# First QKV groups of a four-layer transformer kernel: two row blocks that share weight chunks, batch statistics, earlier border zeros, and a new table of half-steps

## Chip, cores and metric

The kernel runs on one core of one Trainium2 chip. The metric is device time in microseconds (us), taken as the median of several executions. Before the change the three shown executions took 1742.13, 1744.40 and 1746.95 us, so the median is 1744.4 us.

## What is computed

Four layers are applied one after another to x, a matrix of 2048 rows and 640 columns in float32. Layers 0 and 2 are of kind A (attention over eight earlier rows at a stride of 2, 32 heads of 20), layers 1 and 3 of kind B (a Fourier mix over rows and columns, written as matrix products).

```python
x = A_x
x = x + _A_ref(_layernorm(x), A_wqkv, A_wo)
x = x + _B_ref(_layernorm(x), seq_re, seq_im, hid_re, hid_im)
x = x + _A_ref(_layernorm(x), A_wqkv, A_wo)
x = x + _B_ref(_layernorm(x), seq_re, seq_im, hid_re, hid_im)
# _A_ref: qkv = x @ wqkv; softmax over 8 gathered keys; weighted values; @ wo
# _B_ref: seq_re @ (x @ hid_re.T) - seq_im @ (x @ hid_im.T)
```

## The kernel before

Rows are cut into 16 blocks of 128, four chunks c of four blocks j. Every float32 product is made of three passes of fp32r operands (`PASSES`, line 324): each operand is split into a rounded part, hi, and a rest, lo, and the passes are hi·hi, hi·lo and lo·hi. So a split costs a cast and a subtraction for each tile (`split`, line 228; on ScalarE, VectorE or GpSimd), and a group of QKV (one row block by up to 512 columns, 5 chunks k of 128 along the depth) costs 15 matmuls (`qkv_mm`, line 467). A row block gets there by normalisation, five 128x128 transposes on TensorE (`t_pe`, line 327), a cast out of PSUM (`t_hi`, line 336) and a subtraction (`t_lo`, line 340).

`layer_a` (line 348) is ordered by hand on all five engines: a plan of steps -8 to 66 (half-steps: half of a unit of attention each), and in each step a list of phases. The table `CFG` gives for each piece of work its step, and `ph` the order of the phases. Attention products run on VectorE (lines 557, 570, 600) and GpSimd (lines 560, 615 to 617), two half-steps for each of 32 units; TensorE fills in QKV groups, transposes of attention outputs (line 442), subtraction of the hi part in PSUM by a matmul with a negative identity (line 450, `pc_sub`), output products (line 640) and, as the layer runs out, the first products of the next B layer (line 1123, `z_mm`, 15 matmuls for one slab of c, in thirds of 5 that the table `z` places). The B layers' slabs come raw (`cst_in`, transposed on TensorE into `aux` banks) or as they are (`cs_in`). `ln_lo` (line 1046) makes the lo part of the normalised rows of the B layer on VectorE or GpSimd, as the bits `lnv` say.

Before any of that, 18 bf16 matmuls on zeros run on TensorE (line 206). The start of layer 0 is `prologue_first` (line 743). It loads x block 0, weight chunks 0 to 2 of the first QKV group of columns, x block 1, chunks 3 and 4, x blocks 2 and 3, and then the weights of the other three column groups in large pieces (lines 674 and 310), all on the SyncE queue. Then a string `pro` gives the order of small steps: `s` statistics of a block (lines 246 to 252, 274, 280: a reduction on VectorE, squares on ScalarE, a power on GpSimd), `n` normalise (line 293), `H` and `L` hi and lo of a weight chunk (lines 759 and 762; the letter names the engine), `p`, `h`, `l` transposes, cast and subtraction of block 0. The blocks 1 to 3 are transposed in the middle of the groups before them (`mid`, line 474). The border rows of the key and value buffers are zeroed by `zero_rows` (line 736) in the middle of group 1.

Of the kernel before, what the change touches and what calls it, by code (L numbers as in the profile page):

```python
# [13 lines left out]
AF = mybir.ActivationFunctionType  # L14
# [6 lines left out]
D = 640  # L21
# [15 lines left out]
CFG = {'pro': 's0 H0a H2a H1a L0v n0v L1g p0 h0 L2g s1 H3v H4v l0 L3v L4v s2 n1v',  # L37
 'mid0': 's3 n2v',
 'mid0n': 0,
 'mid1': 'n3v',  # L40
 'mid1n': 0,
# [12 lines left out]
 'pad2': 16,  # L54
 'ot': ['ot'],
 'wqg': [0, 0, 0, 0, 0, 0, 0, 1, 1, 1, 0, 1, 0, 1, 1, 0, 1, 0, 1, 0],
 'run': [{'pre': [0, 1, 2, 0, 1, 0, 2, 0, 0, 0, 0, 2, 0, 1, 0, 0],
          'post': [5, 1, 1, 2, 1, 4, 0, 5, 0, 7, 0, 3, 0, 4, 1, 5],
          'y': [[3, 4, 5, 6, 8], [9, 13, 14, 14, 15]]},
         {'pre': [6, 0, 1, 2, 4, 3, 0, 4, 0, 6, 0, 0, 2, 0, 0, 0],  # L60
          'post': [0, 0, 2, 2, 0, 4, 0, 0, 0, 0, 1, 0, 4, 0, 4, 3],
# [13 lines left out]
         'z': [148, 149, 149, 151, 151, 156, 156, 157, 157, 159, 161, 162, 167, 168, 170, 171, 171, 173, 174, 174,  # L75
               175, 175, 175, 176, 178, 179, 180, 180, 181, 184, 186, 186, 187, 187, 188, 188, 191, 193, 194, 198,
# [4 lines left out]
         't2': [48, 48, 48, 48, 52, 51, 52, 52],  # L81
         't3': [57, 58, 60, 60],
         'wst': [0, 0, 0, 0, 0, 0, 0, -1, 0, 1, 0, 0, -1, 1, 0, 0],
         'kvq': [1, 0, 1, 1, 0, 1, 1, 0, 0, 0, 0, 0, 1, 0, 1, 0, 0, 0, 0, 0, 0, 0, 1, 0, 0, 0, 1, 0, 1, 0, 1, 0],
# [5 lines left out]
         'ph': ['evac dma peT0 pe hi z0 fin peL z1 red0 pe2 qk dma2 sA sB red1 sC av0 loE sD sE exp actl evacA sF '  # L90
                'evacO av1 qc dmaw dmac actL lnl pe3w dmar misc clo dmas pe3',
                'peT0 evac dma pe hi z0 peL red0 pe2 z1 fin qk dma2 sA av0 sD sE sB red1 evacA sC loE actL sF evacO '
                'exp dmac av1 actl qc dmas misc clo lnl dmar dmaw pe3 pe3w'],
# [5 lines left out]
         'lnv': [1, 1, 1, 0, 0, 1, 0, 0, 0, 1, 0, 0, 1, 1, 0, 1],  # L99
# [29 lines left out]
         'zla': [0, 0, 2, 0, 1, 0, 1, 1, 1, 1, 0, 1, 0, 2],  # L129
         'ph': ['dma peT0 evac hi red0 pe z0 peL qk z1 fin sA pe2 red1 dma2 sB sD sC av0 loE sE clo evacA exp actl '  # L130
                'actL sF evacO av1 qc dmaw dmas misc pe3 lnl dmar dmac pe3w',
                'peT0 red0 evac pe z0 dma hi fin peL sA z1 qk dma2 pe2 sB red1 av0 sD loE evacA sC sE exp actL evacO '
                'sF av1 dmas dmaw qc actl dmar lnl misc pe3w clo dmac pe3'],
# [3 lines left out]
         'lno': [False, False, True, True],  # L137
# [3 lines left out]
         'tail': 'z68 P H L M2 z67 M3 A2 S2 F2 c14 d14 p14 T2 A3 l2 Z14 z69 S3 F3 c15 d15 p15 T3 l3 G0 G1 G2 Z15 E '  # L141
                 'e0 h0 k0 e1 e2 e3 e4 h1 k1'}],
 'xcr': ['stg', 'sg3', 'sg3']}
TA = 65
NWARM = 18
STG = (-1, "dma2")
NWIN = CFG['nwin']
ZTAGS = ("m0", "m1", "xt", "t0", "t1")
NT = 8
# [19 lines left out]
def tile_layers(ctx: ExitStack, tc: tile.TileContext, x, wqkv, wo, cs, cst, wre, wim, out):  # L169
# [35 lines left out]
    for i in range(NWARM):  # L205
        nc.tensor.matmul(wb, zero[:, :P], zero[:, :512], start=True, stop=True)
# [1354 lines left out]
```

## Time and profile before

| What | Value |
|---|---|
| median of three executions | 1744.4 us |
| the profiled execution | 1743.01 us |
| its span in the trace | 1741.2 us |
| TensorE matmul busy | 1717.2 us, 99% |
| VectorE busy | 1360.1 us, 78% |
| ScalarE busy | 822.6 us, 47% |
| GpSimd busy | 616.1 us, 35% |
| data moved | 419.91 MB, mean 241 GB/s |

The profiled execution lies 1.8 us above its span and 1.4 us below the median. Shares over the whole span mix stages: in layers 0 and 2 VectorE and GpSimd are as full as TensorE, in layers 1 and 3 GpSimd has next to nothing to do. A row of the timeline has a start, a length, the engine, the line, the operation with output and input tiles, its count, and in brackets the idle time of the engine ahead of it with what ended it. A short idle time of TensorE counts as such; the sum of its rows in this profile is about 20 us.

### The profile page before, as it was taken

To read this page: it belongs to the slowest core of one execution; us is meant where nothing else is said; L and a number is where in the kernel's file an instruction comes from. 1 tells how busy PE (TensorE), PEld (TensorE's weight loads), DVE (VectorE), ACT (ScalarE), POOL (GpSimd) and SP (SyncE) were. 2 spreads that over 40 slices of the span, in tenths; PEclk is the share of its full clock that TensorE was granted. 3 is DMA by queue.
4 is the path that set the end of the run, shared out by engine and by line. 5 is a ranking of instruction groups with operands and counts; after the bars stand their busy time and mean duration, and the time that the engine had idled before them with its cause. 6 is when DMAs were issued, how large, how long until landed. Compare 5 with 4: busy or idle time off the path is not lost. (4 is left out here: it accounts for less than half of the span.)

```text
span 1741.2 us, 26545 instructions
## 1 busy us (share of the span) xinstructions
PE 1717.2 (99%) x8828; PEld 1496.2 (86%) x8828; DVE 1360.1 (78%) x2117; ACT 822.6 (47%) x1810; POOL 616.1 (35%) x574
## 2 busy tenths in 40 slices
PE   9999999999999999999999999999999999999999
PEld 6888888788888888888888889888888888888888
DVE  5999999878767767767639998899787677677673
ACT  5655644654445444445534434445444444443441
POOL 4899999950000000000019997899200000000000
PEclk9999999999999999999999999999999999999999
DMA  6786779969787687687548856698598768867861
GB/s 239 245 291 199 209 231 309 323 222 331 264 262 232 215 275 235 206 279 226 189 156 269 273 163 219 213 312 318 179 349 268 256 205 260 257 208 240 264 203 54
DMA packets 266713, 419.91 MB, mean 241 GB/s; under 512 B 22192, under 2 KB 144560, under 8 KB 266320
## 3 DMA queue, kind: packets, MB, share of 16 engines
q1 hardware_dynamic: 251744, 408.38, 71.1%
q10 hardware_dynamic: 14832, 9.83, 1.8%
q8 instruction: 70, 1.15, 0.3%
q14 instruction: 67, 0.55, 0.1%
HBM read 332.99 MB, written 85.14 MB: 240 GB/s over the span
## 5 line engine op out<-in xcount | busy, mean ns | idle before, releaser
L477 PE MATMUL m<-r,s 128*128 128x512 f32 (+1 forms) x1920 | 429.8, 379 | 1.3 <-DVE r L759 0.8
L477 PEld LDWEIGHTS m<-r,s 128*128 128x128 f32 x1920 | 350.2, 188 | 57.5 <-DVE r L759 1.2
L1284 ACT CAST r<-win 128x512 fp32r<-128x512 f32 x242 | 147.1, 620 | 176.1 <-DVE win L1320 103.2
L1190 PE MATMUL aux<-r2a,zo 128*128 128x320 f32 x768 | 226.0, 309 | 0.0
L557 DVE TENSOR_TENSOR pr<-pq,win 128x1280 f32<-128x1280 f32 x128 | 189.8, 1483 | 37.5 <-PE aux L1190 20.3
L615 POOL TENSOR_TENSOR pr<-pr 128x640 f32<-128x640 f32 x126 | 207.5, 1647 | 30.3 <-DVE pr L600 29.1
L1190 PE MATMUL aux<-pr,zo 128*128 128x320 f32 x704 | 208.0, 309 | 0.0
L560 POOL TENSOR_TENSOR pr<-pr 128x640 f32<-128x640 f32 x123 | 176.3, 1433 | 88.4 <-DVE pr L557 88.4
L1285 DVE TENSOR_TENSOR r<-win,r 128x512 fp32r<-128x512 f32 x242 | 162.8, 688 | 38.5 <-ACT r L1284 37.7
L600 DVE TENSOR_TENSOR pr<-pq,win 128x1280 f32<-128x1280 f32 x128 | 190.3, 1488 | 2.6
L280 POOL TENSOR_TENSOR stats<-stats,mhalf 128x1 f32<-128x1 f32 (+1 forms) x31 | 22.1, 714 | 457.9 <-ACT stats L274 457.8
L1291 PE MATMUL m<-r,r 128*128 128x512 f32 x600 | 152.9, 389 | 0.0
L1190 PEld LDWEIGHTS aux<-r2a,zo 128*128 128x128 f32 x768 | 144.2, 188 | 2.2
L1190 PEld LDWEIGHTS aux<-pr,zo 128*128 128x128 f32 x704 | 132.2, 188 | 2.4
L1291 PEld LDWEIGHTS m<-r,r 128*128 128x128 f32 x600 | 112.2, 188 | 23.5 <-DVE r L1285 0.6
L1291 PE MATMUL t<-r,r 128*128 128x512 f32 x492 | 132.0, 390 | 0.0
L616 POOL TENSOR_TENSOR pr<-pr 128x320 f32<-128x320 f32 x126 | 113.1, 897 | 9.9
L570 DVE TENSOR_REDUCE lg<-pr 128x64 f32<-128x640 f32 (+1 forms) x128 | 107.2, 837 | 10.0 <-POOL pr L560 9.7
L1320 DVE TENSOR_TENSOR win<-win,win 128x512 f32<-128x512 f32 x109 | 74.9, 691 | 48.4 <-DMA win<-cs_in 46.8
L1291 PEld LDWEIGHTS t<-r,r 128*128 128x128 f32 x492 | 92.4, 188 | 19.8
L1123 PE MATMUL m<-s,r 128*128 128x512 f32 x348 | 106.7, 394 | 2.0 <-ACT r L1060 0.9
L1123 PE MATMUL t<-s,r 128*128 128x512 f32 x348 | 105.2, 390 | 0.0
(297 smaller groups left out, 3236.1 us busy)
## 6 DMA issues: line engine op xcount, KB each, us to landing
win<-cs_in SPq DMA_DIRECT2D x346, 256.0 KB, 4.1
r<-xc SPq DMA_DIRECT2D x240, 256.0 KB, 4.2
win<-kvb SPq DMA_DIRECT2D x96, 440.0 KB, 4.7
xa<-cs_in SPq DMA_DIRECT2D x120, 256.0 KB, 4.5
win<-kvb SPq DMA_DIRECT2D x64, 360.0 KB, 6.0
xc<-sg SPq DMA_DIRECT2D x28, 512.0 KB, 4.6
xr<-xs SPq DMA_DIRECT2D x40, 320.0 KB, 3.5
kvb<-stg SPq DMA_DIRECT2D x32, 320.0 KB, 2.7
```

What stands on the lines that cost most here:

```text
L477: nc.tensor.matmul(mt[g][:, : GW[q]], st[:, a, k], wq[q][:, b, k], start=n == 0, stop=n == 14)
L557: nc.vector.tensor_tensor(pr, q, wview(u, jp, 0, [[1, FE]]), op=ALU.mult)
L560: nc.gpsimd.tensor_tensor(pv[:, :, 0:10], pv[:, :, 0:10], pv[:, :, 10:20], op=ALU.add)
L570: nc.vector.tensor_reduce(rows(lgs[u], jp), pv.rearrange("p (a h) d -> p a h d", h=HE), axis=AX.X, op=ALU.add,)
L600: nc.vector.tensor_tensor(pr.rearrange("p j w (h d) -> p (j w) h d", d=DH), rows(lgs[u], jp).unsqueeze(3).to_broadcast([P, 2 * W, HE, DH]) ...
L615: g.tensor_tensor(pr[:, :, 0:4], pr[:, :, 0:4], pr[:, :, 4:8], op=ALU.add)
L616: g.tensor_tensor(pr[:, :, 0:2], pr[:, :, 0:2], pr[:, :, 2:4], op=ALU.add)
L1123: self.last = nc.tensor.matmul(self.z[t][k], self.xn[c][:, a, j, k * P : (k + 1) * P], self.ct[s][:, b], start=s == 0 and i == 0, stop=s = ...
L1190: self.last = nc.tensor.matmul(self.ym[e][:, :320], zt[(k, a, ri)][:, j2 * P : (j2 + 1) * P], w[:, e * 320 : (e + 1) * 320], start=(k, a, ...
L1284: nc.scalar.copy(hi, raw)
L1285: nc.vector.tensor_tensor(lo, raw, hi.bitcast(F32), op=ALU.subtract)
L1291: nc.tensor.matmul(bank, w(a, kb), hl[b], start=start and (a, b) == (0, 0), stop=stop and (a, b) == (1, 0),)
```

## The change

Five things are changed together.

- The prologue loads x blocks 0 and 1 first, then weight chunks 0, 3, 1, 2, 4, then x blocks 2 and 3, then the border zeros, then the large weight pieces (`pld`). The zeros get a tile of their own tag.
- Row statistics of layer 0's first four blocks are made by two `bn_stats` on halves of 320 columns and one `bn_aggr` on VectorE, then Ln and Exp of the variance on ScalarE. The reduction, the squares and GpSimd's power go.
- Groups 0 and 1 (row blocks 0 and 1 with the first column group) are no longer run one after the other: `pro` names each of their 30 matmuls (`m0a` is group 0, pass hi·hi, chunk 0; letters a to e are hi·hi, f to j are x hi by weight lo, k to o are x lo by weight hi).
- 15 matmuls on zeros instead of 18.
- Many numbers of the step tables move by one or so: `gs`, `z`, `out`, `wo`, `ph`, `tail` and others of both A layers, the engine bits `wqg` and `lnv`, and `run` and `y` of the B layers.

TensorE's queue, at the start of the program (`t` and `aux` are PSUM banks of the transposes, `m` those of the groups, `pr` the row blocks, `r` the split weights, `s` the transposed blocks; the number behind a name tells tiles apart). Before:

```order
L331 MATMUL t_33_203<-ident_69,pr_13_158 128x128 x2
L331 MATMUL t_34_206<-ident_69,pr_13_158 128x128 x3
L477 MATMUL m_37_233<-r_0_12_157,s_32_202 128x512 x10
L331 MATMUL aux_39_245<-ident_69,pr_18_167 128x128 x2
L331 MATMUL aux_40_248<-ident_69,pr_18_167 128x128 x3
L477 MATMUL m_37_233<-r_0_12_157,s_32_202 128x512 x5
L477 MATMUL m_44_272<-r_0_12_157,s_38_244 128x512 x10
```

And with the change, on the same queue from the same place on:

```order
L350 MATMUL t_38_215<-ident_69,pr_13_155 128x128 x2
L350 MATMUL t_39_218<-ident_69,pr_13_155 128x128 x3
L350 MATMUL aux_41_224<-ident_69,pr_15_157 128x128 x2
L350 MATMUL aux_42_227<-ident_69,pr_15_157 128x128 x3
L804 MATMUL m_43_242<-r_0_12_154,s_37_214 128x512 x2
L804 MATMUL m_44_245<-r_0_12_154,s_40_223 128x512
L804 MATMUL m_43_242<-r_0_12_154,s_37_214 128x512
L804 MATMUL m_44_245<-r_0_12_154,s_40_223 128x512 x3
L804 MATMUL m_43_242<-r_0_12_154,s_37_214 128x512 x4
L804 MATMUL m_44_245<-r_0_12_154,s_40_223 128x512
```

The transposes of block 1 stand ahead of all matmuls of group 0, and the two groups take turns.

VectorE's queue at the start (`stats`, `bns`, `bna` hold statistics, `win` the raw weight chunks). Before:

```order
L246 TENSOR_REDUCE stats_189<-pr_13_158 128x1
L247 TENSOR_SCALAR stats_189<-stats_189 128x1
L762 TENSOR_TENSOR r_0_12_157<-win_160,r_0_12_157 128x512
L293 TENSOR_SCALAR pr_13_158<-pr_13_158,stats_189 128x640
L246 TENSOR_REDUCE stats_189<-pr_18_167 128x1
L247 TENSOR_SCALAR stats_189<-stats_189 128x1
L759 CAST r_0_12_157<-win_169 128x512
L759 CAST r_0_12_157<-win_171 128x512
```

And with the change, from the same place on:

```order
L260 BN_STATS bns_198<-pr_13_155 128x6 x2
L261 BN_AGGR bna_199<-bns_198 128x2
L260 BN_STATS bns_203<-pr_15_157 128x6 x2
L261 BN_AGGR bna_204<-bns_203 128x2
L270 TENSOR_SCALAR pr_13_155<-pr_13_155,bna_199,stats_185 128x640
L270 TENSOR_SCALAR pr_15_157<-pr_15_157,bna_204,stats_185 128x640
L361 TENSOR_TENSOR s_37_214<-t_38_215,s_37_214 128x256
L361 TENSOR_TENSOR s_37_214<-t_39_218,s_37_214 128x384
```

Both blocks are now normalised before any weight chunk is touched on VectorE; the lo part of chunk 0 has gone to GpSimd.

TensorE's queue near the end of layer 0, where slabs of the next layer (`stg`) and attention outputs (`zo`) are transposed between thirds of `z_mm` (five matmuls each; `wa` and `s` are slabs that are split). Before, transposes first and two thirds behind them:

```order
L442 MATMUL aux_585_3695<-ident_69,zo_520_3259 128x128 x3
L442 MATMUL aux_587_3697<-ident_69,stg_3667 128x128 x4
L1123 MATMUL m_496_3155<-wa_3645,r_1_539_3391 128x512
L1123 MATMUL m_497_3156<-wa_3645,r_1_539_3391 128x512
L1123 MATMUL xt_3157<-wa_3645,r_1_539_3391 128x512
L1123 MATMUL t_499_3158<-wa_3645,r_1_539_3391 128x512
L1123 MATMUL t_500_3159<-wa_3645,r_1_539_3391 128x512
```

With the change, the end of the second of these thirds, and what follows it:

```order
L1162 MATMUL t_512_3186<-wa_3599,r_1_544_3394 128x512
L461 MATMUL aux_590_3708<-ident_69,zo_527_3269 128x128 x3
L461 MATMUL aux_592_3710<-ident_69,stg_3675 128x128 x4
L469 MATMUL aux_590_3708<-s_589_3707,nident_74 128x384
L469 MATMUL aux_592_3710<-s_591_3709,nident_74 128x512
```

The transposes stand two thirds later, and the subtractions (now line 469) follow them at once.

The diff, cut to its core:

```diff
@@ CFG @@
-CFG = {'pro': 's0 H0a H2a H1a L0v n0v L1g p0 h0 L2g s1 H3v H4v l0 L3v L4v s2 n1v',
- 'mid0': 's3 n2v',
...
+CFG = {'pro': 'b0 b1 f0 n0 f1 H0a p0 n1 p1 H1a h0 l0 L0g h1 l1 H2a m0a m0k m1a m0l H4v m1k m1b m1c H3a L1g m0m b2 m0f m0d '
+        'L3g m0c m1o m0b L2v m1d m1l f2 m0e m1f m1m m1n m0o m1e m0g n2 p2 L4v b3 m0i m0j m0h m0n m1i m1h h2 m1g m1j '
+        'f3 n3 l2',
...
- 'pad2': 16,
+ 'pad2': 64,
...
- 'wqg': [0, 0, 0, 0, 0, 0, 0, 1, 1, 1, 0, 1, 0, 1, 1, 0, 1, 0, 1, 0],
+ 'wqg': [0, 0, 0, 0, 0, 0, 0, 0, 0, 1, 0, 1, 1, 1, 1, 0, 1, 0, 1, 0],
...
-         'lnv': [1, 0, 1, 0, 0, 0, 1, 0, 1, 1, 0, 1, 1, 1, 1, 1],
+         'lnv': [0, 0, 1, 0, 0, 0, 1, 0, 1, 1, 0, 0, 1, 1, 0, 1],
...
+ 'nwarm': 15,
+ 'pld': 'x0 x1 k0 k3 k1 k2 k4 x2 x3 z0',
+ 'mid2': 'p3 h3 l3'}
@@ Stats @@
+        def batch(self, j, xt):
+            b = T([P, 2, nc.vector.BN_STATS_DIM], "bns", bufs=2)
+            a = T([P, nc.vector.BN_AGGR_DIM], "bna", bufs=4)
+            for h in range(2):
+                nc.vector.bn_stats(b[:, h], xt[:, h * 320 : (h + 1) * 320])
+            nc.vector.bn_aggr(a, b)
+            self.mv[j] = a
+
+        def batch_fin(self, j):
+            r = self.rstd[:, j : j + 1]
+            nc.scalar.activation(r, self.mv[j][:, 1:2], AF.Ln, bias=eps)
+            nc.scalar.activation(r, r, AF.Exp, scale=-0.5)
@@ zero_rows @@
-            zrow = wtile([4, (W - 1) * FE])
+            zrow = T([4, (W - 1) * FE], "xr")
@@ prologue_first @@
-            for j, (k0, k1) in enumerate(((0, 3), (3, 5))):
-                if j:
+            for j in range(NJ):
+                if j == 1:
                     T([P, CFG["pad2"]], "pad2")
-                x_load(0, j, f"pr{j}")
-                for k in range(k0, k1):
-                    wq[(0, k)] = wq_load1(0, k)
...
+            for t in CFG["pld"].split():
+                n = int(t[1])
+                if t[0] == "z":
+                    zero_rows()
+                elif t[0] == "k":
+                    wq[(0, n)] = wq_load1(0, n)
...
+            def qmm(j, i, k):
+                a, b = PASSES[i]
+                g = j
+                if count[g] == 0:
+                    mt[g] = pt([P, 512], f"m{g % 2}")
+                nc.tensor.matmul(
+                    mt[g][:, : GW[0]], xnT[(0, j, 1)][:, a, k], w0[:, b, k], start=count[g] == 0, stop=count[g] == 14
+                )
+                count[g] += 1
...
-            mid[1] = m[: CFG["mid1n"]] + xt_all(2, "t") + m[CFG["mid1n"] :] + [(zero_rows, ())]
-            mid[2] = xt_all(3, "aux")
+            mid[2] = [(step, (t,)) for t in CFG["mid2"].split()]
```

More of the change, by code (lines that the diff above doesn't have):

```diff
@@ L204, in tile_layers @@
     wb = pt([P, 512], "m1")
-    for i in range(NWARM):
+    for i in range(CFG["nwarm"]):
         nc.tensor.matmul(wb, zero[:, :P], zero[:, :512], start=True, stop=True)
@@ L240, in __init__ @@
             self.done = set()
+            self.mv = {}
             self.sums = st[:, 8:16].rearrange("p (a j) -> p a j", a=2)
@@ L467, in qkv_mm @@
         def qkv_mm(g, cqj):
+            if first and g < 2:
+                return
             c, q, j = cqj
@@ L786, in step @@
                 elif t[0] == "p":
-                    both(lambda c, j, i: xt_pe(c, j, i, f"t{i}"), 0)
+                    both(lambda c, j, i: xt_pe(c, j, i, f"{('t', 'aux')[j % 2]}{i}"), n)
                 elif t[0] == "h":
-                    both(xt_hi, 0)
-                else:
-                    both(xt_lo, 0)
+                    both(xt_hi, n)
+                elif t[0] == "l":
+                    both(xt_lo, n)
+                else:
+                    for x in e:
+                        i, k = divmod("abcdefghijklmno".index(x), KD)
+                        qmm(n, i, k)
             for t in CFG["pro"].split():
                 step(t)
-            m = [[step, (t,)] for t in CFG["mid0"].split()]
-            mid[0] = m[: CFG["mid0n"]] + xt_all(1, "aux") + m[CFG["mid0n"] :]
-            m = [[step, (t,)] for t in CFG["mid1"].split()]
-            mid[1] = m[: CFG["mid1n"]] + xt_all(2, "t") + m[CFG["mid1n"] :] + [(zero_rows, ())]
-            mid[2] = xt_all(3, "aux")
+            assert count[:2] == [15, 15]
+            mid[2] = [(step, (t,)) for t in CFG["mid2"].split()]
             for i in range(KD):
```

103 lines of the change are left out of this document (54 added, 49 removed), and 14 rows, old and new, of the table CFG.

## The prediction, as it went on record

> **What bounds the kernel now.** I read the page's busy times first, then the windows by stage, then all waits of TensorE. The page's chain of work only reaches back to the middle of the span, so the early stages are read from their windows.
>
> ```profile
> PE 1717.2 (99%) x8828; PEld 1496.2 (86%) x8828; DVE 1360.1 (78%) x2117; ACT 822.6 (47%) x1810; POOL 616.1 (35%) x574
> 0.00:10.00 10.00, 8.01 (x27) 3.33 (x27) 4.99 (x12) 6.13 (x14) 3.88 (x13) 1.00 0.85 302
> 10.00:20.00 10.00, 8.17 (x37) 6.10 (x38) 7.47 (x17) 4.98 (x15) 2.55 (x5) 1.00 0.80 321
> 60.00:360.00 300.00, 292.59 (x1563) 258.14 (x1563) 281.20 (x412) 166.56 (x445) 279.04 (x258) 1.00 0.79 261
> ```
>
> TensorE is busy for 1717.2 of 1741.2 us, at a granted clock of 1.00 (the column behind POOL). No edit takes a real matmul away, so only waits can go: the 24 us without work. The first 20 us leave TensorE 3.8 us idle, part of its early busy time being matmuls on zeros. From 60 to 360 us (most of layer 0) VectorE (281.20 of 300) and GpSimd (279.04) are nearly as full as TensorE (292.59): there a shorter wait of TensorE may only make it wait for them.
>
> **The prologue.** The timeline of TensorE up to the first gapless stretch:
>
> ```profile
> 7.72 0.76 PE L331 MATMUL t<-ident,pr 128*128 128x128 f32 x5 [0.37 <-DVE pr L293]
> 8.61 1.21 PE L477 MATMUL m<-r,s 128*128 128x512 f32 x4
> 10.58 1.19 PE L477 MATMUL m<-r,s 128*128 128x512 f32 x4 [0.76 <-DVE r L759]
> 11.97 1.10 PE L477 MATMUL m<-r,s 128*128 128x512 f32 x2 [0.20 <-DVE r L762]
> 14.02 0.77 PE L331 MATMUL aux<-ident,pr 128*128 128x128 f32 x5 [0.94 <-DVE pr L293]
> 18.07 0.71 PE L331 MATMUL t<-ident,pr 128*128 128x128 f32 x5
> 18.53 2.56 PE L477 MATMUL m<-r,s 128*128 128x512 f32 x10
> 21.39 33.44 PE L477 MATMUL m<-r,s 128*128 128x512 f32 x145
> ```
>
> 145 matmuls take 33.44 us, 0.2306 each; five transposes hold TensorE for 18.53 − 18.07 = 0.46. At 21.39 groups 0 to 3 still lack 25 matmuls, so the first column group ends at 21.39 + 25 × 0.2306 = 27.16 us. Its work is 60 × 0.2306 + 4 × 0.46 = 15.7 us; begun at 7.72 it could have ended at 23.4. So 3.7 us are stalls: block 0 alone can't use a chunk before it is split, and block 1 is normalised only at 13.96.
>
> The rows for the new order's times:
>
> ```profile
> 1.31 6.04 PE L206 MATMUL m<-s 128*128 128x512 bf16 x18 [1.31 <-DVE s L203]
> 5.46 1.39 PEld L206 LDWEIGHTS <-s 128*128 128x128 bf16 x7 [0.18 <-issue]
> 3.71 0.82 DVE L246 TENSOR_REDUCE stats<-pr 128x1 f32<-128x640 f32 x1 [2.38 <-DMA pr<-x_in]
> 4.56 0.15 DVE L247 TENSOR_SCALAR stats<-stats 128x1 f32<-128x1 f32 x1
> 283.87 0.48 DVE L258 SCALAR_TENSOR_TENSOR xa<-aux,xa 128x320 f32<-128x320 f32 x1
> 5.70 0.20 ACT L274 ACTIVATE stats<-stats 128x1 f32<-128x1 f32 x1
> 5.81 1.64 ACT L759 CAST r<-win 128x512 fp32r<-128x512 f32 x3
> 7.05 0.61 DVE L293 TENSOR_SCALAR pr<-pr,stats 128x640 f32<-128x640 f32 x1
> 8.19 0.81 ACT L338 CAST s<-t 128x256 fp32r<-128x256 f32 x2 [0.74 <-PE t L331]
> 10.45 0.88 DVE L342 TENSOR_TENSOR s<-t,s 128x256 fp32r<-128x256 f32 x2
> 7.53 2.71 POOL L762 TENSOR_TENSOR r<-win,r 128x512 fp32r<-128x512 f32 x2 [0.97 <-ACT r L759]
> ```
>
> `bn_stats` isn't in this trace. Its bounds are the one-column row (0.15) and the whole 640-column reduction (0.82); I take half of that reduction, 0.42, close to the 320-column row of 0.48. `bn_aggr` I put at 0.15, at most 0.30. A block's statistics then cost 2 × 0.42 + 0.15 = 1.0 us of VectorE, as before (0.82 + 0.15), but the squares on ScalarE and the power on GpSimd go; Ln and Exp cost 2 × 0.20.
>
> What the loads allow, by windows of 1 us (the last column is GB/s, thousandths of a MB per us), and the two rows of the zeros before:
>
> ```profile
> 1.00:2.00 1.00, 0.69 (x2) 0.28 (x3) 0.32 (x2) 1.00 (x1) 0.38 (x4) 1.00 0.35 36
> 2.00:3.00 1.00, 1.00 (x4) 0.31 (x3) 0.00 (x0) 0.41 (x3) 0.00 (x0) 1.00 0.74 242
> 3.00:4.00 1.00, 1.00 (x4) 0.44 (x3) 0.29 (x1) 0.00 (x0) 0.00 (x0) 1.00 1.05 388
> 4.00:5.00 1.00, 1.00 (x4) 0.30 (x2) 0.68 (x2) 0.25 (x1) 0.00 (x0) 1.00 1.05 307
> 5.00:6.00 1.00, 1.00 (x5) 0.45 (x4) 0.00 (x0) 0.97 (x4) 0.01 (x1) 1.00 0.99 353
> 6.00:7.00 1.00, 1.00 (x7) 0.39 (x4) 0.56 (x1) 1.00 (x3) 0.56 (x1) 1.00 1.03 390
> 18.57 0.56 POOL L738 MEMSET win<- 4x560 f32 x1
> 19.15 2.67 SPq L741 DMA_DIRECT2D kvb<-win  x8
> ```
>
> 0.67 MB have moved by 4.0: blocks 0 and 1 (0.33 MB each). Block 0's consumer starts 0.6 us after its bytes at that rate; so block 1 is there at 4.6, chunk 0 at 5.4, chunk 1 (1.44 MB) at 6.9, the last chunk near 8.2. The zeros' memset (0.56) now stands on GpSimd ahead of the identity's last step, which the transposes need only at 6.75. Their eight issues (2.67) move on SyncE ahead of the large loads, to about 4.6 to 7.3; until 9 us the queue still has the same 2.6 MB of blocks and chunks to move, which hides that delay. Without that cover the large pieces land 2.7 us later, and the second column group needs the first of them only at 23.7.
>
> So: statistics of block 0 end at 4.7, of block 1 at 5.7, Ln and Exp of each 0.5 later; block 0 is normalised 5.7 to 6.35, block 1 until 7.0 (before: 7.66 and 13.96). Seven weight loads of the zeros take 1.39, so three fewer end TensorE's warm-up at 7.35 − 0.6 = 6.75; there the transposes of block 0 start, 0.97 earlier than now. ScalarE casts chunks 0 and 1 until 7.5, block 0 until 8.3, block 1 until 9.1, chunk 2 until 9.7, chunk 3 until 10.2. TensorE starts group 0 at 7.95 and then takes a matmul from whichever group has its operands: about 1.2 us of waits until 10 us, none behind. Chunk 4 (VectorE, 10.5), the lo parts (GpSimd 8.3, 9.6 and 11.6; VectorE 12.3 and 13.6) and block 2 (13 us; needed at 13.5) each come before their turn. With 15.7 us of work from 6.75 and 1.2 of waits, the first column group ends at 23.7. **Gain: 27.16 − 23.7 = 3.4 us.** Bounds: `bn_stats` at 0.82 delays block 1 by 1.6 and more `bn_aggr`, 0.3 more, leaving 1.5; at 0.15 the warm-up holds the transposes at 6.75 anyway, and with every stall gone the gain is 0.97 + 3.7 = 4.7. The first attention product waits for the same groups, so VectorE's and GpSimd's long stretch shifts with TensorE.
>
> **The step table.** Waits of TensorE whose cause the new order moves:
>
> ```profile
> 87.20 0.50 PE L450 MATMUL xt<-s,nident 128*128 128x512 f32 x1 [0.68 <-ACT s L446]
> 108.39 0.66 PE L442 MATMUL xt<-ident,xa 128*128 128x128 f32 x4 [0.92 <-ACT xa L297]
> 287.33 0.66 PE L442 MATMUL aux<-ident,zo 128*128 128x128 f32 x4 [0.46 <-ACT wa L465]
> 325.94 0.63 PE L442 MATMUL aux<-ident,stg 128*128 128x128 f32 x4 [1.69 <-DMA stg<-cst_in]
> 334.95 0.50 PE L450 MATMUL aux<-s,nident 128*128 128x512 f32 x1 [0.68 <-ACT s L446]
> 1156.88 0.50 PE L450 MATMUL aux<-r,nident 128*128 128x256 f32 x2 [1.57 <-ACT r L446]
> ```
>
> At 87.20 and 334.95 a group or a third now stands between transposes and subtraction; at 287.33 a third stands ahead of the transposes; at 325.94 they stand two thirds (2.3 us) later, longer than the load was late. Together 0.68 + 0.46 + 1.69 + 0.68 = 3.5. At the moved place of 325.94 the subtraction follows its transposes at once, as at 334.95 before: 0.68 back, with a third of `z_mm` queued behind it on TensorE and, behind that, nothing but TensorE's own stream. So 2.8. The waits at 108.39 and 1156.88 (2.5 together) also lose their neighbours, but both end with ScalarE's queue, which follows VectorE there: I count nothing. Bounds: nothing, since VectorE and GpSimd are as full; and all 6.0.
>
> **Sum.** 3.4 + 2.8 = 6.2. The profiled execution's 1743.0 (1741.2 of span and 1.8 around it) becomes 1736.8; the median lies 1.4 higher, so 1738.2. Pads, tags and other moved numbers I put at nothing: they change neither the count of matmuls nor any row above, and small waits both ways are inside the bounds.
>
> **Rivals.** Those about VectorE and GpSimd rest on these rows:
>
> ```profile
> 1140.00:1160.00 20.00, 17.95 (x102) 15.46 (x101) 19.04 (x29) 9.66 (x30) 18.98 (x19) 1.00 0.95 322
> L1048 POOL TENSOR_TENSOR r<-r,r x10: 1569/1578/1589, 307.9 to 1201.2; 128x640 fp32r<-128x640 f32 x10
> L759 DVE CAST r<-win x2: 591/1054/1518, 8.5 to 9.0; 128x512 fp32r<-128x512 f32 x2
> ```
>
> - *The table gains nothing.* TensorE's saved waits come back as waits for VectorE or GpSimd at the end of each A layer. For it: both near 94% from 60 to 360 us. Against: the removed waits end with ScalarE or a load. Only the prologue's 3.4 stay: 1741.0.
> - *The table gains all 6.0*: 9.4 off, 1735.0.
> - *GpSimd becomes the bound in layer 2, and the kernel is slower.* `lnv` moves three lo parts there from VectorE to GpSimd at 1.58 us each, 4.7 in all. At 1140 to 1160 GpSimd has 1.0 us free in 20, so three within some 80 us just pass what is free (about 4). It decides once that free time can't be used, because GpSimd's idle moments are waits for VectorE. If the last attention outputs then wait for all of it and the table gains nothing, 4.7 − 3.4 = 1.3 us slower: 1745.7. Against: VectorE, the fuller one (19.04), is relieved.
> - *VectorE and GpSimd get in each other's way in the prologue.* Two casts on VectorE beside GpSimd's subtraction took 0.59 and 1.52, so an overlap can cost 0.93. With the change three subtractions on GpSimd lie beside VectorE's statistics; three such delays, 2.8, leave 0.6 of 3.4 there: 1741.0.
>
> The Trainium skill ("SBUF — State Buffer", "Who interferes with whom") says that the two engines share a port pair which one of them locks for a whole instruction. By that rule the last rival holds wherever VectorE's instruction takes both pairs; the cast of 1.52 agrees, no row here shows it for `bn_stats`. By the rule the time would be 1741.0, by the forecast's reading, in which those instructions run beside each other, 1738.2.
>
> **How the numbers follow.** Forecast 0.55; table nothing 0.18; table all 0.13; prologue collisions 0.06; GpSimd bound 0.08. Two terms' bounds give 1744.4 − 10.7 = 1733.7 to 1744.4 − 1.5 = 1742.9; a median of three whose runs lie 4.8 apart adds about one each way: **1732.5 to 1744.0**. A measurement tells 0.3%, 5.2 us, from no change. The forecast lies 1 us past that edge: two thirds of its chance, all of "table all" and little of the rest make faster 0.52; slower by that needs 8.6 us of losses against the 3.4: 0.04; within, 0.44.
>
> **What would show it.** Right: the gapless stretch of groups begins near 16 us and the first column group ends near 23.7; `bn_stats` near 0.42; no wait for the raw slab near 323; the first attention product 3.4 earlier. Wrong: chunk 1 later than 7.5, `bn_stats` near 0.8, the layer-1 products starting no earlier than the prologue's gain allows, or GpSimd full up to the end of layer 2.

## The result, and the profile after

| Kernel | median, us | range, us | executions | ratio to before, 95% interval |
|---|---|---|---|---|
| before | 1742.65 | 1741.54 to 1746.95 | 7 | |
| changed | 1737.14 | 1736.35 to 1740.75 | 7 | 0.9967 (0.9957 to 0.9976) |
| changed, once more | 1738.08 | 1736.95 to 1738.33 | 6 | 0.9968 (0.9955 to 0.9980) |

The change gains 5.5 us by the first comparison, 0.33%. The forecast was 1738.2, a gain of 6.2 us: 1.1 us above the measured median and inside the range of 1732.5 to 1744.0. Its base, the median of three (1744.4), lies 1.75 us above that of seven.

The first profiled execution of the changed kernel was the slowest of its seven, 1740.75 us. The repeat's profiled execution took 1736.95 us, so I read the terms from that one and call it the second trace. (The profiled execution of the run with the table alone took 1825.91 us at a mean granted clock of 0.889; it is left out of the comparisons, and its trace isn't read.) Its TensorE in the prologue, to be held against the timeline that the prediction shows:

```profile
1.31 4.79 PE L206 MATMUL m<-s 128*128 128x512 bf16 x15 [1.31 <-DVE s L203]
6.47 0.74 PE L350 MATMUL t<-ident,pr 128*128 128x128 f32 x5 [0.37 <-DVE pr L270]
7.11 0.77 PE L350 MATMUL aux<-ident,pr 128*128 128x128 f32 x5
8.17 5.69 PE L804 MATMUL m<-r,s 128*128 128x512 f32 x22 [0.30 <-ACT s L357]
...
17.80 22.42 PE L498 MATMUL m<-r,s 128*128 128x512 f32 x97
```

The matmuls on zeros end at 6.10, and TensorE waits 0.37 us for block 0. Both blocks are transposed one behind the other, 22 matmuls of the two groups follow, and at 17.80 the first four groups lack 25 matmuls, as before at 21.39. At 22.42/97 = 0.231 us each the first column group ends at 23.58 (before 27.16). VectorE in the same stretch:

```profile
3.72 0.89 DVE L260 BATCH_NORM_STATS2 bns<-pr 128x6 f32<-128x320 f32 x2 [2.40 <-DMA pr<-x_in]
4.64 0.21 DVE L261 BATCH_NORM_AGGREGATE bna<-bns 128x2 f32<-128x12 f32 x1
...
5.76 1.30 DVE L270 TENSOR_SCALAR pr<-pr,bna,stats 128x640 f32<-128x640 f32 x2
...
10.13 0.88 DVE L260 BATCH_NORM_STATS2 bns<-pr 128x6 f32<-128x320 f32 x2
...
11.18 0.95 DVE L790 TENSOR_TENSOR r<-win,r 128x512 fp32r<-128x512 f32 x1
...
12.57 0.68 DVE L790 TENSOR_TENSOR r<-win,r 128x512 fp32r<-128x512 f32 x1
```

`bn_stats` takes 0.44 (half of 0.89) and `bn_aggr` 0.21; both blocks are normalised by 7.06 (before 7.66 and 13.96).

Next, one and the same place of TensorE's stream in both traces, first in that of before, then in the second trace:

```profile
58.66 0.50 PE L450 MATMUL xt<-s,nident 128*128 128x512 f32 x1 [0.68 <-ACT s L446]
374.32 2.18 PE L640 MATMUL aux<-r2a,zo 128*128 128x320 f32 x12 [0.46 <-ACT zo L446]
1232.60 2.18 PE L640 MATMUL aux<-r2a,zo 128*128 128x320 f32 x12 [0.46 <-ACT zo L446]
```

```profile
54.94 0.50 PE L469 MATMUL xt<-s,nident 128*128 128x512 f32 x1 [0.68 <-ACT s L465]
369.55 2.17 PE L661 MATMUL aux<-r2a,zo 128*128 128x320 f32 x12 [0.46 <-ACT zo L465]
1226.30 2.17 PE L661 MATMUL aux<-r2a,zo 128*128 128x320 f32 x12 [0.46 <-ACT zo L465]
```

The lead is 3.72 us behind the prologue, 4.77 at layer 0's last output products, 6.30 at those of layer 2, and 6.0 in the spans (1741.2 and 1735.2). So in this pair of traces the prologue gave 3.7 us, the table 1.05 in layer 0 and 1.5 in layers 1 and 2; how far other traces bear that out stands near the end. Where the first 1.05 comes from, and what it was reduced by, stands in the waits of the second trace:

```profile
101.98 5.47 PE L498 MATMUL m<-r,s 128*128 128x384 f32 x30 [1.55 <-ACT sg L513]
301.56 0.66 PE L461 MATMUL aux<-ident,stg 128*128 128x128 f32 x4 [1.55 <-DVE r L277]
1151.65 0.38 PE L469 MATMUL aux<-ot,nident 128*128 128x256 f32 x1 [0.38 <-ACT ot L465]
1158.25 4.66 PE L661 MATMUL aux<-r2a,s 128*128 128x320 f32 x30 [1.08 <-DVE r L277]
```

All the waits that the prediction named are gone or shrunk (at 87.20, 108.39, 287.33, 325.94, 334.95, and 1156.88 from 1.57 to 0.38 at 1151.65). The wait of 0.68 us that the prediction put back behind the moved transposes of the raw slab isn't there either: the subtraction starts at 324.50 with none. Two others have come: 1.55 us at 102, where none was, and 1.55 at 302, where before had 0.22. The second is read from two engines at the same place. Before:

```profile
299.94 4.56 PE L640 MATMUL aux<-r2a,s 128*128 128x320 f32 x30
304.17 0.48 DVE L258 SCALAR_TENSOR_TENSOR r<-aux,r 128x320 f32<-128x320 f32 x1
```

and in the second trace:

```profile
295.35 4.66 PE L661 MATMUL aux<-r2a,s 128*128 128x320 f32 x30
301.02 0.48 DVE L277 SCALAR_TENSOR_TENSOR r<-aux,r 128x320 f32<-128x320 f32 x1
```

TensorE starts these products 4.59 us earlier, VectorE reads their sums 3.15 us earlier. VectorE is busy for 18.53 of the 20 us from 280 on (18.71 before), so what TensorE saved beyond 3.15 it now waits for.

The slow first execution differs by one clear stretch, here its row and its window (the columns behind GpSimd's busy time are the granted clock, the DMA share and GB/s):

```profile
302.04 0.92 PE L461 MATMUL aux<-ident,stg 128*128 128x128 f32 x4 [1.89 <-DVE r L277]
302.62 1.20 PE L1162 MATMUL m<-s,r 128*128 128x512 f32 x2
```

```profile
302.00:306.00 4.00, 3.48 (x10) 2.37 (x10) 2.63 (x4) 1.03 (x2) 3.84 (x4) 0.57 1.04 400
```

Behind a wait of 1.89 us two matmuls took 1.20 us instead of 0.63, at a granted clock of 0.57 in the mean of these 4 us and of 0.50 in the windows of 1 us at 303 and 304. That execution was 0.48 us behind the second trace at this row (302.04 and 301.56) and 1.92 at the next output products (306.20 and 304.28): 1.4 us lost.

### The profile page after: what moved, and what is told of

Read it like the earlier page. It is cut to its first block, busy times and chain, and to the rows that moved or that the text cites. A ratio compares the mean times of both kernels' runs of the same rounds, so it can differ in the third digit from the quotient of the medians.

```text
span 1739.0 us, 26552 instructions
## 1 busy us (share of the span) xinstructions
PE 1717.6 (99%) x8825; PEld 1497.1 (86%) x8825; DVE 1354.7 (78%) x2118; ACT 823.9 (47%) x1815; POOL 615.4 (35%) x570
## 4 chain that ended last, share of the span: by engine, by line
PE 83%; DVE 7%; DMA 4%; issue 2%; POOL 2%; ACT 2%; SPq 0%; ACTq 0%; DVEq 0%; POOLq 0%
PE m L498 16%; PE aux L1229 16%; PE t L1330 11%; PE m L1330 11%; PE aux L661 6%; PE pq L1330 5%; PE xt L1330 5%; PE m L1162 4%; PE t L1162 4%; DVE pr L578 2%; PE xt L1162 2%; DVE pr L621 2%; DMA win<-kvb 1%; DMA win<-cs_in 1%; POOL pr L636 1%
## 5 line engine op out<-in xcount | busy, mean ns | idle before, releaser
L498 PE MATMUL m<-r,s 128*128 128x512 f32 (+1 forms) x1890 | 422.0, 378 | 1.9 <-ACT sg L513 1.9
L498 PEld LDWEIGHTS m<-r,s 128*128 128x128 f32 x1890 | 344.6, 188 | 56.3 <-ACT sg L513 3.3
```

What stands on the lines that cost most here:

```text
L498: nc.tensor.matmul(mt[g][:, : GW[q]], st[:, a, k], wq[q][:, b, k], start=n == 0, stop=n == 14)
```

## The experiments

The theory was the forecast's: prologue 3.4 and table 2 to 3, independent of each other. The rivals: one of the parts is all of it, and inside the prologue either the statistics or the sharing is all of it. Times of one group of four runs share a chip; "before" is the median of before there.

**Runs 1 to 4** (before 1743.62 us, 25 executions).

*The prologue alone.* The tables `run` and `ly` of before in the changed kernel.

```diff
- 'run': [{'pre': [3, 1, 2, 0, 1, 0, 2, 0, 0, 0, 0, 2, 0, 1, 0, 0],
+ 'run': [{'pre': [0, 1, 2, 0, 1, 0, 2, 0, 0, 0, 0, 2, 0, 1, 0, 0],
...
```

> The changed prologue with the step table of before (the tables 'run' and 'ly'). Theory: the two parts add up, so this kernel keeps the prologue's 3.4 us and lacks the table's share: 3.4 us below before (ratio 0.9980), 2.1 us above the changed kernel, and TensorE's waits of before at about 87, 108, 287, 326 and 335 us come back, each 3.5 us earlier. Rival 1: the prologue is all of it and the table gains nothing: 5.5 us below before (0.9968). Rival 2: the table is most of it and the prologue's lead is lost again behind full VectorE and GpSimd: less than 1.5 us below before (over 0.9991).

Measured: 1739.24 us (8 executions), ratio 0.9974 (0.9964 to 0.9984), 4.4 us below before. On its trace:

```profile
54.96 0.50 PE L469 MATMUL xt<-s,nident 128*128 128x512 f32 x1 [0.68 <-ACT s L465]
83.53 0.50 PE L469 MATMUL xt<-s,nident 128*128 128x512 f32 x1 [0.68 <-ACT s L465]
104.34 0.66 PE L461 MATMUL xt<-ident,xa 128*128 128x128 f32 x4 [0.54 <-ACT xa L316]
321.33 0.63 PE L461 MATMUL aux<-ident,stg 128*128 128x128 f32 x4 [0.72 <-DMA stg<-cst_in]
```

The waits of before are back, 3.7 us earlier at first (58.66 − 54.96) and 4.6 at the raw slab. The time lies between the theory and rival 1; its interval (2.8 to 6.3 us) excludes rival 2 only. The raw slab's wait is 0.72 instead of 1.69 with no step of it moved, so its size isn't fixed by the table. With this small wait the trace reaches the last output products of layer 0 at 369.64, only 0.09 us behind the second trace (369.55); at those of layer 2 it is 2.3 behind (1228.60 and 1226.30). That is so although the clock fell near 283 here too, and four transposes took 1.11 us instead of 0.66:

```profile
283.25 1.11 PE L461 MATMUL aux<-ident,zo 128*128 128x128 f32 x4 [0.46 <-ACT wa L484]
284.00:288.00 4.00, 4.00 (x16) 3.29 (x15) 4.00 (x4) 2.61 (x9) 2.80 (x4) 0.72 0.91 247
```

The waits ahead of it were short: 0.85 us at 280.42, 0.39 at 282.06 and this 0.46.

*The table alone.* `run` and `ly` of the changed kernel in the kernel before, the same edit the other way round.

> The prologue of before with the changed step table. Theory: 2.1 to 2.8 us below before (ratio 0.9984 to 0.9988), the waits at 87, 108, 287, 326 (the raw slab) and 335 us gone. Rival 1 (table gains nothing): equal to before within 0.5 us (0.9997 to 1.0003). Rival 2 (table is most): 4 us or more below before (under 0.9977).

Measured: 1741.30 us (11 executions), ratio 0.9989 (0.9980 to 0.9998), 0.3 to 3.5 us below before. The median is 2.3 below, near the theory; rival 1 lies at one end of the interval, rival 2 outside the other. 4.4 and 2.3 add to 6.7, which their intervals don't tell from the whole 5.5. The other way round, the changed kernel measured beside it (the next run) lies only 1.2 us below the prologue alone.

*The changed kernel once more*, unchanged.

> The changed kernel once more, for a second profiled execution. In the first one, the slowest of its seven, TensorE waited 1.89 us for VectorE at 302 us and then ran at a granted clock of 0.57 until 306. Theory: that stretch belongs to that execution, so here the clock is 1.00 throughout, the wait near 302 is shorter than 1 us, and the profiled execution lies at 1737 us. Rival: the wait at 302 is made by the new table and stands in every execution; then the clock falls there again and the seven agree only by chance.

Measured: 1738.08 us, the profiled one 1736.95; the clock is 1.00 in that stretch, but the wait of 1.55 at 302 stays. Each half of the expectation is right once: the low clock belonged to the first execution, the wait to the table.

*The old statistics in the new order.*

```diff
-CFG = {'pro': 'b0 b1 f0 n0 f1 H0a p0 n1 p1 H1a h0 l0 L0g h1 l1 H2a m0a m0k m1a m0l H4v m1k m1b m1c H3a L1g m0m b2 m0f m0d '
+CFG = {'pro': 's0 s1 n0 H0a p0 n1 p1 H1a h0 l0 L0g h1 l1 H2a m0a m0k m1a m0l H4v m1k m1b m1c H3a L1g m0m s2 m0f m0d '
...
```

> The changed kernel with the row statistics of before (whole reduction on VectorE, squares on ScalarE, power on GpSimd) in place of the batch statistics, everything else as changed. Theory: VectorE needs the same 1.0 us for each block, but the two squares (0.83 each, with their read-out 0.92) come back ahead of ScalarE's casts, so block 0 is normalised 0.6 us later, block 1 about 1.3 us later, and the first column group ends at 24.4 to 25.0 instead of 23.7: 0.7 to 1.3 us above the changed kernel. Rival 1: ScalarE has room (it waits 0.37 us for a chunk anyway), no difference within 0.3 us. Rival 2: the statistics carry the prologue's gain: 2.5 us or more above, the first column group near 26.5.

Measured: 1742.84 us (11 executions), ratio 0.9991 (0.9982 to 1.0000): nearly all of the prologue's gain is lost, rival 2. TensorE, then VectorE on its trace:

```profile
9.34 0.77 PE L350 MATMUL aux<-ident,pr 128*128 128x128 f32 x5 [1.25 <-DVE pr L312]
58.70 0.50 PE L469 MATMUL xt<-s,nident 128*128 128x512 f32 x1 [0.68 <-ACT s L465]
```

```profile
6.66 0.61 DVE L312 TENSOR_SCALAR pr<-pr,stats 128x640 f32<-128x640 f32 x1 [0.95 <-POOL stats L299]
7.72 1.55 DVE L312 TENSOR_SCALAR pr<-pr,stats 128x640 f32<-128x640 f32 x1 [0.46 <-POOL stats L299]
14.31 1.58 DVE L312 TENSOR_SCALAR pr<-pr,stats 128x640 f32<-128x640 f32 x1 [1.23 <-POOL stats L299]
```

The place of 54.94 is reached at 58.70, as before. My 1.3 us for block 1 left out two things: VectorE now waits for GpSimd's power, and the normalisation then falls beside GpSimd's subtraction (2.76 us from 7.66 on) and takes 1.55 instead of 0.61. Block 1 is ready at 9.27 instead of 7.06, block 2 at 15.89 instead of 12.65.

**Runs 5 to 8** (before 1742.36 us, 30 executions).

*No sharing, batch statistics kept.* The names `m1a` to `m1o` are put behind the last `m0`.

```diff
-CFG = {'pro': 'b0 b1 f0 n0 f1 H0a p0 n1 p1 H1a h0 l0 L0g h1 l1 H2a m0a m0k m1a m0l H4v m1k m1b m1c H3a L1g m0m b2 m0f m0d '
...
+CFG = {'pro': 'b0 b1 f0 n0 f1 H0a p0 n1 p1 H1a h0 l0 L0g h1 l1 H2a m0a m0k m0l H4v H3a L1g m0m b2 m0f m0d L3g m0c '
+        'm0b L2v f2 m0e m0o m0g n2 p2 L4v b3 m0i m0j m0h m0n m1a m1k m1b m1c m1o m1d m1l m1f m1m m1n m1e m1i '
+        'm1h m1g m1j h2 f3 n3 l2 ',
```

> The changed kernel, but the 15 matmuls of block 1's first group stand behind those of block 0's: nothing shared, the batch statistics kept. Theory: block 0 alone has to wait for the split of each chunk, whose last lo part ends at 13.4 us; from 8.3 us to there stand 15 matmuls (3.5 us) instead of 22, so about 1.7 us of waits come, the first column group ends near 25.4, and the kernel is 1.5 to 2 us above the changed one. Rival 1: sharing is worth nothing once block 1 is early (within 0.4 us of the changed kernel). Rival 2: sharing is all of the prologue's gain (3.4 us or more above).

Measured: 1740.30 us (11 executions), ratio 0.9987 (0.9978 to 0.9995). That is 1.5 and 2.4 us above the two runs of this group that turn out to cost nothing (1738.83 and 1737.93).

```profile
9.90 2.16 PE L804 MATMUL m<-r,s 128*128 128x512 f32 x8 [0.41 <-ACT r L787]
12.96 0.74 PE L350 MATMUL t<-ident,pr 128*128 128x128 f32 x5 [0.90 <-DVE pr L270]
56.73 0.50 PE L469 MATMUL xt<-s,nident 128*128 128x512 f32 x1 [0.67 <-ACT s L465]
```

56.73 − 54.94 = 1.79 us, as the theory has it. But this execution's matmuls on zeros took 6.31 us, and its first transposes start at 7.45 instead of 6.47. Against the run on `lnv` below, whose transposes start at 7.45 too and which reaches the place at 55.60, it is 1.13. So the sharing is worth 1.1 to 1.8 us, and both rivals fall. It fills the time in which block 0 alone waits for a chunk's split.

*Batch statistics in the kernel before.*

```diff
                 if t[0] == "s":
-                    x_stats(0, n, True)
-                    x_fin(0, n)
+                    if n == 0:
+                        stats[0] = Stats()
+                    stats[0].batch(n, xnT[(0, n)])
+                    stats[0].batch_fin(n)
```

> The kernel before with batch statistics and Ln and Exp in place of its row statistics, its order of steps unchanged. Theory: in that order block 0's normalisation stands behind the split of chunk 0 and block 1's behind five other steps of VectorE, so the earlier statistics help little: first column group 0 to 0.6 us earlier, 0 to 0.6 us below before (ratio 0.9996 to 1.0000). Rival: the statistics carry the gain alone, as their removal from the changed kernel cost 3.6 us on its trace: 3 us or more below before (under 0.9983).

Measured: 1744.29 us (11 executions), ratio 1.0010 (1.0001 to 1.0019), 0.2 to 3.3 us above before. The rival falls, and my sign was wrong too. The trace shows the prologue unchanged, and the loss elsewhere:

```profile
58.78 0.50 PE L469 MATMUL xt<-s,nident 128*128 128x512 f32 x1 [0.68 <-ACT s L465]
326.25 1.08 PE L461 MATMUL aux<-ident,stg 128*128 128x128 f32 x4 [2.27 <-DMA stg<-cst_in]
```

```profile
326.00:328.00 2.00, 1.75 (x7) 1.59 (x8) 1.33 (x1) 1.60 (x5) 1.92 (x3) 0.57 0.91 351
```

58.78 against 58.66: nothing gained. Near 326 the raw slab is waited for 2.27 us, and the clock falls behind it (0.57 in the 2 us shown). All 11 executions have a mean clock of 0.998 or 0.999; of before's 30, 13 have less than 1.000. Why the slab came later here isn't shown.

*The zeros back behind the first groups.*

```diff
- 'pld': 'x0 x1 k0 k3 k1 k2 k4 x2 x3 z0',
+ 'pld': 'x0 x1 k0 k3 k1 k2 k4 x2 x3',
...
-            mid[2] = [(step, (t,)) for t in CFG["mid2"].split()]
+            mid[2] = [(step, (t,)) for t in CFG["mid2"].split()] + [(zero_rows, ())]
```

> The changed kernel with the border zeros behind the first three groups again, behind the large weight loads. Theory: the zeros are hidden at both places; the large pieces land earlier and ScalarE's wait of 0.6 us for the first of them at 16.8 us goes, but TensorE starts the gapless stretch and the first attention product within 0.2 us of the changed kernel: same time within 0.5 us. Rival: the eight issues (5.4 us of SyncE) ahead of the large loads cost something that later waits hide, and this kernel is 1 us or more faster. Second rival: behind the large loads the zeros hold up the first loads of the windows, 1 us or more slower.

Measured: 1738.83 us (11 executions), ratio 0.9977 (0.9968 to 0.9986). Its gapless stretch starts 0.3 us later than in the second trace and the place of 54.94 is at 55.53; the next run, with the zeros unmoved, has 55.60 there. So the zeros cost nothing that the trace shows.

*The bits `lnv` of layers 2 and 3 put back.*

```diff
-         'lnv': [0, 0, 1, 0, 0, 0, 1, 0, 1, 1, 0, 0, 1, 1, 0, 1],
+         'lnv': [1, 0, 1, 0, 0, 0, 1, 0, 1, 1, 0, 1, 1, 1, 1, 1],
```

> The changed kernel with one row of the table put back: in layers 2 and 3 three lo parts of the normalised rows go from GpSimd to VectorE again. The wait of TensorE for ScalarE of 1.57 us (1156.88 us of before) has shrunk to 0.38 in the changed kernel, although I had counted nothing there. Theory: relief of VectorE did it, so that the wait comes back with 1.2 to 1.6 us near 1152, and the kernel is 1.0 to 1.5 us slower. Rival: the order of the half-steps did it, and nothing changes within 0.3 us on the trace.

Measured: 1737.93 us (8 executions), ratio 0.9974 (0.9964 to 0.9984), and the same 0.40 us in place of 0.38:

```profile
1152.05 0.39 PE L469 MATMUL aux<-ot,nident 128*128 128x256 f32 x1 [0.40 <-ACT ot L465]
```

The rival: VectorE's relief had no part in it. With it goes the prediction's rival of a full GpSimd: three lo parts there or on VectorE make no difference.

**Runs 9 to 12** (before 1743.63 us, 19 executions).

*One pair of stores back on SyncE.*

```diff
-         'kvq': [1, 0, 1, 1, 0, 0, 1, 0, 0, 0, 0, 1, 1, 0, 1, 0, 0, 0, 0, 0, 0, 0, 0, 0, 0, 0, 1, 0, 1, 0, 1, 0],
+         'kvq': [1, 0, 1, 1, 0, 0, 1, 0, 0, 0, 0, 0, 1, 0, 1, 0, 0, 0, 0, 0, 0, 0, 0, 0, 0, 0, 1, 0, 1, 0, 1, 0],
```

> The changed kernel with one pair of stores (near 95 us) moved from ScalarE's DMA queue back to SyncE's, as before. In the changed kernel TensorE waits 1.55 us at 102 us for ScalarE, which itself waits 1.60 us for the landing of a store of the two staging buffers. Theory: the two stores on two queues at once land late; with both on SyncE the wait at 102 goes, the one of before for ScalarE's normalisation near 107 comes back with 0.5 to 0.9, and TensorE is 0.5 to 1.0 us earlier at 112 us; at the end 0.3 to 1.0 us faster. Rival: the half-steps of VectorE and GpSimd set that place, TensorE waits as long for something else, no difference within 0.2 us on the trace at 112 us.

Measured: 1736.81 us (5 executions), ratio 0.9962 (0.9950 to 0.9974). ScalarE, which TensorE waits for, first in the second trace, then here with TensorE's row:

```profile
101.28 0.56 ACT L512 COPY stg<-m 128x480 f32<-128x480 f32 x1 [1.60 <-DMA qb<-stg]
```

```profile
99.72 0.56 ACT L512 COPY stg<-m 128x480 f32<-128x480 f32 x1 [0.25 <-DMA qb<-stg]
100.42 5.48 PE L498 MATMUL m<-r,s 128*128 128x384 f32 x30 [0.18 <-ACT sg L513]
279.31 0.63 PE L461 MATMUL aux<-ident,zo 128*128 128x128 f32 x4 [1.00 <-DVE xa L277]
```

The wait at 102 is gone, and none has come in its place. At 279.31 the lead over the second trace (280.86) is 1.55 us, of which 0.22 stood before 102 already, so 1.33 is this one bit's: more than I expected. It is the fastest median of all kernels here, but not told apart from the changed kernel's by the intervals: waits of single executions in layer 1 (0.86 us at 558 here) take as much. At the last output products of layer 2 this trace and the second stand level (1226.35 and 1226.30).

*The wait for the raw slab filled, in the kernel before.*

```diff
-         'kw': {'pc_sub 62': 2, 'pc_pe 50': 2},
+         'kw': {'pc_sub 62': 2, 'pc_pe 50': 2, 'pc_pe 58 1': 6},
```

> The kernel before with six more matmuls on zeros (0.23 us each, 1.4 us) in TensorE's wait of 1.69 us for the raw slab near 326 us. In another kernel that wait grew to 2.27 us, and the four us behind it ran at a granted clock of 0.57. Theory: such a wait lets the clock fall in a part of the executions of before (those with a mean clock of 0.999 or less lie about 2 us above the others), so with the wait filled nearly all executions have 1.000, the highest lies below 1744.5, and the median falls by 0.5 to 1.5 us, although no wait of the program gets shorter. Rival: the fall of the clock has nothing to do with that wait; as many executions with 0.999 or less as before, and the median the same or up to 0.5 us higher for the added work.

Measured: 1744.12 us (12 executions), ratio 1.0006 (0.9997 to 1.0016). Five of 12 have a mean clock of 0.999, against 5 of 19 of before beside it.

```profile
325.67 0.63 PE L442 MATMUL aux<-ident,stg 128*128 128x128 f32 x4 [0.60 <-DMA stg<-cst_in]
```

The wait is filled, and neither the share of low clocks nor the time falls: the rival. That all 11 executions with batch statistics have a low mean clock fits the wait of 2.27 us in the one trace of that kernel; whether the others had that wait isn't shown. The wait of 1.69 us in before isn't what scatters its times. What does stays open.

*The thirds of layers 2 and 3 put back.*

```diff
-         'z': [148, 148, 150, 150, 152, 152, 154, 155, 161, 162, 164, 167, 168, 168, 169, 170, 171, 171, 171, 174,
+         'z': [148, 148, 150, 151, 151, 152, 155, 160, 161, 162, 164, 168, 168, 169, 169, 170, 171, 171, 173, 174,
...
-         'zla': [0, 0, 2, 0, 1, 0, 0, 1, 0, 0, 0, 1, 1, 2],
+         'zla': [0, 0, 2, 0, 1, 0, 1, 1, 1, 1, 0, 1, 0, 2],
```

> The changed kernel with the places of the output's thirds in layers 2 and 3 (and the leads of their loads) put back. There the changed table moves one third (five matmuls, 1.14 us) ahead of the transposes that wait for ScalarE at 1157 us of before. Theory: ScalarE is there at the same time in both kernels and the third merely fills the wait, so the wait comes back with 1.2 to 1.6 us, and TensorE is 1.0 to 1.4 us later at 1196 us, the kernel as much slower. Rival 1: other moved half-steps freed ScalarE there, no difference within 0.3 us. Rival 2: the third is given back as a longer wait for VectorE at 1158 us (1.08 us in the changed kernel), a difference under 0.4 us.

Measured: 1738.86 us (6 executions), ratio 0.9973 (0.9962 to 0.9984).

```profile
1139.14 0.44 PE L469 MATMUL xt<-ot,nident 128*128 128x384 f32 x1 [0.24 <-ACT ot L465]
1153.25 0.39 PE L469 MATMUL aux<-ot,nident 128*128 128x256 f32 x1 [1.72 <-ACT ot L465]
1160.18 4.66 PE L661 MATMUL aux<-r2a,s 128*128 128x320 f32 x30 [0.26 <-DVE r L277]
```

The wait for ScalarE is back with 1.72 (0.38 in the changed kernel), and the wait for VectorE behind it falls from 1.08 to 0.26. From 1139.14 to 1160.18 are 21.04 us; in the second trace from 1137.84, where the same row stands, to 1158.25 only 20.41. In this pair the moved third fills the wait for ScalarE (1.34 less), 0.82 of that is given back at VectorE, and 0.63 is left. The two waits are as in the second trace in the seven other traces with the third in its new place (0.38 to 0.61 and 1.08 to 1.09), but the stretch between the two rows takes 20.53 to 21.57 us there, so the 21.04 can't be told from them. The theory's wait came back; the theory's loss of 1.0 to 1.4 isn't shown, and rival 2 (under 0.4) fits better.

*The store on SyncE, and the wait at 302 filled with five matmuls on zeros.*

```diff
-         'kw': {'pc_sub 62': 2, 'pc_pe 50': 2},
+         'kw': {'pc_sub 62': 2, 'pc_pe 50': 2, 'pc_pe 54': 5},
```

> The changed kernel with the stores near 95 us on SyncE as in the run beside it, and with five matmuls on zeros (1.15 us) in TensorE's wait of 1.55 us for VectorE near 302 us, behind which the first profiled execution of the changed kernel ran at a clock of 0.57. Theory: the matmuls cost nothing, as the wait is longer, and take away the last place at which the clock falls: all executions at 1.000, at or up to 0.5 us below the kernel with the stores alone. Rival: the added matmuls end after VectorE is ready in some executions, 0.3 to 1 us above it.

Measured: 1737.74 us (6 executions), ratio 0.9966 (0.9955 to 0.9978), all executions at a clock of 1.000, but so were all without the filling. The median is 0.9 above that run's, which their ranges (1736.46 to 1738.32, 1736.36 to 1737.44) don't tell apart from noise: no gain. On the traces TensorE is 0.72 us behind that run's at 280.03 (279.31 there) and 1.01 behind it past the wait (303.57 and 302.56), so the added matmuls cost 0.3 us here, the rival's lower edge.

## Why the prediction was right, and where it wasn't

**The prologue: forecast 3.4, measured 3.7 in the second trace.** Eight traces with batch statistics and shared groups reach the place of 58.66 between 54.72 and 55.60, so 3.1 to 3.9 us, 3.4 in the mean. The working holds nearly row by row: `bn_stats` 0.44 (0.42), blocks normalised by 7.06 (7.0), the first column group ends at 23.58 (23.7), VectorE's first attention product starts at 33.47 instead of 37.18. Where it strayed the terms were small: `bn_aggr` 0.21 (0.15), chunk 1 at 7.23 (6.9), group 0 at 8.17 (7.95). The waits, forecast as 1.2 us until 10, are 1.2 us from 6.47 to 13.70 (7.23 us less two sets of transposes of 0.46 and 22 matmuls of 0.231), only 0.45 of it among the matmuls. One step was wrong: the warm-up was to hold the transposes until 6.75, but in this trace it ended at 6.10, and they waited for block 0's normalisation. The 15 matmuls on zeros take 4.79 to 6.31 us in the traces, the 18 of before 5.48 to 6.07; why they differ the traces don't show.

SyncE's queue, in the second trace:

```profile
5.05 5.29 SPq L762 DMA_DIRECT2D kvb<-xr  x8
10.39 0.83 SPq L695 DMA_DIRECT2D r2a<-wqkv_in  x2
```

The zeros' eight issues took 5.29 us instead of 2.67, and the large loads left at 10.39; the run with the zeros put back shows that this was hidden too.

What I had not seen is how the parts depend on each other. Statistics alone gain nothing (58.78 against 58.66), the new order with its sharing alone nothing (58.70), both together 3.1 to 3.9. Sharing needs block 1 early; early blocks need an order that uses them.

**The table: forecast 2.8, measured 1.05 + 1.5 in one pair of traces, about 2 over more.** From the place of 58.66 to the last output products of layer 2 before takes 1173.94 us, and the same in the run with the slab's wait filled. The traces of the new table without a fall of the clock (the second, old statistics, no sharing, late zeros, `lnv` put back) take 1171.13 to 1172.80, so the table gives 1.1 to 2.8 us, 2.1 in the mean. With the prologue's 3.4 that is the measured 5.5. To the end of layer 0 these five take 314.36 to 314.61, before 315.66, the prologue alone 314.68: there the gain is 0.1 to 1.3 us, as the old table's waits happen to fall.

That the sum came near is partly luck, for its parts aren't right. In layer 0 the four removals came, and more: the 0.68 that I put back isn't there, and the 0.92 at 108.39, for which I counted nothing, went too. Two steps failed the other way. "Pads, tags and other moved numbers I put at nothing": one of those numbers sends a pair of stores over ScalarE's queue, and the staging buffers come free later; taking it back was worth 1.33 us of TensorE's place in layer 0. And at 302 TensorE waits for VectorE: the new table had brought TensorE 0.9 us beyond the prologue's 3.7 there and left VectorE 0.6 short of it (4.59 and 3.15). Every trace of the new table without a filling has this wait, 1.21 us or more, and no trace of the old one more than 0.26; which of the moved numbers makes it is not separated. It is the rival "the table gains nothing", true at this one place. In layer 2 I counted nothing for 1156.88, because the wait ends with ScalarE. It still does, but a third now fills it, and most of that comes back as the wait for VectorE behind it. Where the 1.5 comes from I have not separated.

**The rivals.** "The table gains all 6.0" lies outside the interval of the table alone (0.3 to 3.5 us). GpSimd as the bound in layer 2 is refuted by the run on `lnv`. Collisions in the prologue: two `bn_stats` beside GpSimd's subtraction (10.13) took 0.88 like the others, so they don't collide; one subtraction of VectorE (11.18) took 0.95 instead of 0.68, and the path hid it. The Trainium skill ("SBUF — State Buffer", "Who interferes with whom") has GpSimd share one port pair with VectorE under an exclusive lock. The normalisation of 1.55 instead of 0.61 in the run with old statistics agrees.

## What to carry to other kernels

Ask of each part of a prologue what the next one does with its earliness: here two parts were worth nothing alone and 3.4 us together. A step moved into a wait of TensorE gains only up to the next place where TensorE waits for the fuller engine; hold that engine's lead against TensorE's there, row against row. Of a table of small numbers, those that choose a queue need a look at what waits for the landing.

## What the runs showed of the hardware

- In three traces the granted clock fell to 0.50 (windows of 1 us) for about 3.4 us, and the matmuls took up to twice as long: behind a wait of 1.89 us, behind one of 2.27, and behind three short ones of 0.85, 0.39 and 0.46. Single waits of 1.81 us (old statistics, at 106), 1.79 (the prologue alone, at 461) and 1.55 left it at 1.00, so the length of one wait alone doesn't decide. The Trainium skill ("TensorE: Matmul & The Clock Gate", "Part 1: The HAM clock gate") puts the fall behind an idle window of about 3.4 us, at half rate. The half rate agrees, and these waits were shorter than such a window.
- A normalisation of 640 columns on VectorE took 0.61 us alone and 1.55 and 1.58 beside a subtraction on GpSimd; `bn_stats` beside one was not slowed.
- A pair of stores on ScalarE's queue beside SyncE's own: the older store's buffer came free at 101.28, against 99.72 with all of them on SyncE. Why it lands later the traces don't show.
- Executions of one kernel lie up to 5.9 us apart (before, 25 executions), with the slab's wait filled 7.9 (12 executions). Part of that is the clock (1.4 us lost in the changed kernel's first execution), part waits of 0.5 to 1.8 us in layers 1 and 3 that stand in one trace and not in another.
